# A fused attention, expert mixture and bilinear kernel on one Trainium2 core: the first expert in wider blocks, and a first list ordered against a clock

## The chip, the cores and the metric

One Trainium2 chip, one of its cores. The metric is the device time of one execution in microseconds; the kernel before was timed three times: 2153.72, 2157.41 and 2157.93, median 2157.41. Engines are called PE (TensorE, matmuls), DVE (VectorE), ACT (ScalarE), POOL (GpSimd) and SP (the queue that issues most DMAs).

## The reference

```python
def _attn_ref(q, k, v, f_logit):            # 4 batches, 8 heads, 768 steps, head size 48
    f = 1.0 / (1.0 + np.exp(-f_logit))
    for t in range(S):
        state = f[:, :, t, :, None] * state + np.einsum('bhd,bhe->bhde', k[:, :, t], v[:, :, t])
        y[:, :, t] = np.einsum('bhd,bhde->bhe', q[:, :, t], state)

def _moe_ref(x, w_gate, w1, w2):            # x: 3072 x 384, 8 experts, 1024 wide
    logits = x @ w_gate
    P = np.exp(logits - logits.max())
    for _ in range(8):
        P /= P.sum(1, keepdims=True) + 1e-09
        P /= P.sum(0, keepdims=True) + 1e-09
        P *= N / E
    for e in range(E):
        out += P[:, e:e + 1] * (np.maximum(x @ w1[e], 0.0) @ w2[e])

def _moe2_ref(x, w_a, w_b, w_out):          # 384 -> 1536 -> 384
    return (x @ w_a) * (x @ w_b) @ w_out
```

The three run one after the other: the attention's output, 3072 tokens of 384, is the mixture's x, and the mixture's output the bilinear layer's.

## The kernel before, in words

Everything is float32. A product is made of three matmuls: each operand is split in a part `hi` (a ScalarE copy into the type float32r) and what remains, `lo` (a subtraction on DVE or POOL), and the three are hi x hi, hi x lo, lo x hi. `gemm_f` (L508) is x times the first weights, `gemm_t` and `gemm_d` (L522, L533) are the second GEMM with the tokens or the model dimension on the output's partitions.

The program is two lists of operations. Each operation is put down by `Plan.add` (L106) with a priority, an engine, an estimated duration, the keys it reads and writes, and a function that issues its instructions; the list is then ordered by a planner that plays the engines through, and issued in that order. Each engine works off its own instructions strictly in that order.

The first list (`plan` of L596, ordered by `order`, L132, at L1150) holds 24 attention steps of 128 tokens (`attention`, L624), and as filler for PE the first expert without its last 128 hidden columns (`expert0`, L862): 7 hidden tiles, in blocks of 256 tokens (`EB`, L557). Block b can start when steps 2b and 2b+1 have left x as hi and lo (`b_x`, L575 to L580, two buffers). Per block the first GEMM is 7 x 9 matmuls of 256 columns; the second is 42 matmuls of 384 columns in blocks 0 to 3 and 63 of 256 columns in the others (`TURNED`). Each hidden tile leaves its PSUM bank by two ScalarE copies and one POOL subtraction (L875, L878, L880). `order` lets filler run on PE in a share of 0.6 to attention's matmuls. Until the first filler PE gets `spare` matmuls (L917) that compute nothing of use. Also in the first list: the splits of expert 0's weights (`add_piece`, L494: a DMA into one of two `raw` tiles, a ScalarE copy, a POOL subtraction), the gate's logits of one tile of 128 tokens (`logits`, L847: six matmuls with 16 or 8 columns), sums of x for the later stage (`x_make`, L1102), five x tiles (`x_take`, L1131), and the weights of the second list's jobs 0 and 1 (`w1_load`, `w1_split`, L1017 and L1047: raw blocks into `stage`, 13 sums, three splits into `w1t[0]` or `w1t[1]`).

The second list (`plan` of L1159, ordered by `timed`, L239) is the rest: the mixture's jobs and the bilinear layer's, 81 jobs of 45 matmuls of 512 columns in `front` (L1235), in 15 groups of three, and the second GEMMs in `back` and `back_turned`. `timed` plays its list through by `listed` (L270) with durations of its own, moves what held PE up to the front and keeps the best of 60 passes. At its start stand what the first list left of expert 0 (block 10's second GEMM and block 11), the last tile's logits, and the Sinkhorn rounds (`sinkhorn`, L929), eight times a matmul, a DVE column scaling (L960 to L962) and a row scaling. x tiles 9 to 14 and the hidden parts of later jobs share memory (`er`) with expert 0's tiles and wait for it by `guard`.

## Time and profile before

| | us |
|---|---|
| three timed runs | 2153.72, 2157.41, 2157.93 |
| profiled execution | 2153.39 |
| its span, first to last instruction | 2151.6 |
| PE busy | 2134.3 |
| DVE busy | 1720.0 |
| POOL busy | 1184.4 |
| ACT busy | 940.9 |

The profile is one execution of its own; its time stands beside its span, which leaves out what lies before the first and behind the last instruction. Busy times overlap. A matmul's own duration in a row is longer than what it costs, since matmuls run into each other: the distance from one row's start to the next is the cost.

### The profile page before, as it was taken

To read this page: it belongs to the slowest core of one execution; us is meant where nothing else is said; L and a number is where in the kernel's file an instruction comes from. 1 tells how busy PE (TensorE), PEld (TensorE's weight loads), DVE (VectorE), ACT (ScalarE), POOL (GpSimd) and SP (SyncE) were. 2 spreads that over 40 slices of the span, in tenths; PEclk is the share of its full clock that TensorE was granted. 3 is DMA by queue.
4 is the path that set the end of the run, shared out by engine and by line. 5 is a ranking of instruction groups with operands and counts; after the bars stand their busy time and mean duration, and the time that the engine had idled before them with its cause. 6 is when DMAs were issued, how large, how long until landed. Compare 5 with 4: busy or idle time off the path is not lost.

```text
span 2151.6 us, 41006 instructions
## 1 busy us (share of the span) xinstructions
PE 2134.3 (99%) x15371; PEld 1869.3 (87%) x15371; DVE 1720.0 (80%) x2882; ACT 940.9 (44%) x1761; POOL 1184.4 (55%) x1106
## 2 busy tenths in 40 slices
PE   8999999999999999999999999999999999999999
PEld 8999999989989999988888888888888888888888
DVE  7878888377878777698888986899998887866656
ACT  3544454454444445444444444444343445533331
POOL 2212121268877666477787767755545688535322
PEclk9999999999999999999999999999999999999999
DMA  6546644356675567865657678777665766878552
GB/s 133 116 106 165 166 112 98 109 203 241 235 254 196 185 223 267 279 227 194 219 179 232 198 273 279 243 255 247 226 199 174 239 218 228 302 232 283 172 173 74
DMA packets 340951, 438.66 MB, mean 204 GB/s; under 512 B 148024, under 2 KB 224656, under 8 KB 337296
## 3 DMA queue, kind: packets, MB, share of 16 engines
q1 hardware_dynamic: 326016, 422.40, 60.9%
q10 hardware_dynamic: 14736, 13.64, 1.9%
q8 instruction: 121, 1.98, 0.4%
q14 instruction: 78, 0.64, 0.1%
HBM read 295.58 MB, written 135.64 MB: 200 GB/s over the span
## 4 chain that ended last, share of the span: by engine, by line
PE 96%; DVE 3%; DMA 1%; issue 0%; ACT 0%; SPq 0%; DVEq 0%
PE pG L1258 28%; PE pR L539 21%; PE pR L528 18%; PE pF L1258 10%; PE pM L516 4%; PE pM L539 2%; PE pT L654 1%; PE pM L528 1%; PE pA L697 1%; PE pM L917 1%; PE pO L810 1%; PE pA L709 1%; PE pA L741 1%; PE pO L816 1%; PE pO L782 1%; DVE z L1539 1%
## 5 line engine op out<-in xcount | busy, mean ns | idle before, releaser
L539 PE MATMUL pR<-er 128*128 128x512 f32 (+1 forms) x2178 | 537.8, 383 | 0.0
L1258 PE MATMUL pG<-xs,w 128*128 128x512 f32 x1701 | 469.0, 392 | 3.6 <-DVE z L1539 3.0
L539 PEld LDWEIGHTS pR<-er 128*128 128x128 f32 x2178 | 401.1, 188 | 80.5
L528 PE MATMUL pR<-er 128*128 128x384 f32 x2232 | 433.8, 336 | 0.0
L1539 ACT ACTIVATE z<-pG 128x512 f32<-128x512 f32 x397 | 237.2, 598 | 437.5 <-PE pG L1258 370.5
L528 PEld LDWEIGHTS pR<-er 128*128 128x128 f32 x2232 | 397.6, 188 | 23.9
L1258 PEld LDWEIGHTS pG<-xs,w 128*128 128x128 f32 x1701 | 315.9, 188 | 64.3 <-DVE z L1539 3.2
L1539 POOL TENSOR_TENSOR er<-z,er 128x512 fp32r<-128x512 f32 x177 | 246.5, 1400 | 195.9 <-ACT er L1539 135.2
L1539 POOL TENSOR_TENSOR acc<-acc,tmp 128x512 f32<-128x512 f32 x168 | 232.4, 1390 | 173.3 <-DVE tmp L1539 172.3
L1539 ACT ACTIVATE er<-z 128x512 fp32r<-128x512 f32 x353 | 217.6, 628 | 212.4 <-PE pR L539 123.8
L1258 PE MATMUL pG<-er,w 128*128 128x512 f32 x972 | 276.5, 393 | 2.8 <-DVE z L1539 2.6
L1539 DVE TENSOR_TENSOR z<-pF,z 128x512 f32<-128x512 f32 x268 | 182.2, 684 | 64.4 <-PE pF L1258 42.8
L880 POOL TENSOR_TENSOR er<-l,er 128x256 fp32r<-128x256 f32 x84 | 74.6, 891 | 282.3 <-ACT l L878 234.5
L1258 PEld LDWEIGHTS pG<-er,w 128*128 128x128 f32 x972 | 180.9, 188 | 36.5 <-DVE z L1539 4.7
L1539 DVE TENSOR_TENSOR z<-z,pG 128x512 f32<-128x512 f32 x206 | 140.4, 682 | 63.5 <-PE pG L1258 61.9
L1539 POOL TENSOR_TENSOR stage<-stage 128x128 f32<-128x128 f32 x325 | 168.7, 551 | 19.8 <-DMA stage<-in_moe_w_dram 18.2
L1539 DVE SCALAR_TENSOR_TENSOR er<-z,er 128x512 fp32r<-128x512 f32 x150 | 146.6, 986 | 7.4 <-ACT er L1539 7.1
L1539 DVE SCALAR_TENSOR_TENSOR acc<-pR,prob,acc 128x384 f32<-128x384 f32 x168 | 100.5, 611 | 63.0 <-PE pR L528 60.6
L486 POOL TENSOR_TENSOR er<-raw,er 128x384 fp32r<-128x384 f32 (+1 forms) x82 | 94.4, 1159 | 101.8 <-ACT er L484 96.8
L1539 POOL TENSOR_TENSOR w<-stage,w 128x512 fp32r<-128x512 f32 (+2 forms) x75 | 125.0, 1677 | 38.4 <-ACT w L1539 33.5
L1258 PE MATMUL pF<-er,w 128*128 128x512 f32 x486 | 138.8, 394 | 0.0
L1258 PE MATMUL pF<-xs,w 128*128 128x512 f32 x486 | 136.8, 391 | 0.0
(283 smaller groups left out, 3227.0 us busy)
## 6 DMA issues: line engine op xcount, KB each, us to landing
er<-w2d SPq DMA_DIRECT2D x138, 384.0 KB, 4.4
wfmoe<-w SPq DMA_DIRECT2D x19, 1920.0 KB, 7.2
w<-wfmoe SPq DMA_DIRECT2D x38, 768.0 KB, 5.3
w2d<-er SPq DMA_DIRECT2D x69, 384.0 KB, 4.2
w<-wfmoe SPq DMA_DIRECT2D x38, 640.0 KB, 5.6
w<-wfmoe SPq DMA_DIRECT2D x38, 512.0 KB, 4.8
wfout<-w SPq DMA_DIRECT2D x8, 1920.0 KB, 7.7
raw<-in_moe_w_dram SPq DMA_DIRECT2D x64, 192.0 KB, 2.6
```

Of the source, the lines that this page charges most:

```text
L486: plan.add(prio + 1, "POOL", S_COST[0] + m * S_COST[1], [gk, key], [key], lambda: nc.gpsimd.tensor_tensor(out=lj, in0=got, in1=f32(hj), op ...
L516: nc.tensor.matmul(out=ps, lhsT=a[:, kk, fs], rhs=b[:, kk, :], start=(i == 0), stop=(i == 3 * KD - 1),)
L528: nc.tensor.matmul(out=ps, lhsT=a[:, off:off + 128], rhs=b, start=(start and i == 0), stop=(stop and i == n - 1))
L539: nc.tensor.matmul(out=ps, lhsT=a[:, d * 128:d * 128 + 128], rhs=b, start=(start and i == 0), stop=(stop and i == n - 1))
L654: nc.tensor.transpose(ps[0:R, p * 128:p * 128 + 128], src[:, p * 128:p * 128 + R], ident)
L697: nc.tensor.matmul(out=A0[o:o + 64, w, :], lhsT=pct(bk)[r, g, :], rhs=pct(bq)[r, g, :])
L709: nc.tensor.matmul(out=A1[o:o + 56, 0, w, :].rearrange("j (b e) -> j b e", e=8), lhsT=pct(k3)[r, g, 0:56], rhs=qv[r, g, :, 1, :])
L741: nc.tensor.matmul(out=A1[o:o + 48, 1, w, :].rearrange("j (b e) -> j b e", e=16), lhsT=pct(k3)[r, g, 0:48], rhs=qv[r, g, :, 1, :])
L782: nc.tensor.matmul(out=ps[64 * hd:64 * hd + m, p * D:(p + 1) * D], lhsT=kn[64 * c:64 * c + 64, p * R + 64 * hd:p * R + 64 * hd + m], rhs=b ...
L880: op(POOL, .76, [f"hh{ft}", kf], [f"hl{ft}"], lambda hh=hh, hl=hl, hf=hf: nc.gpsimd.tensor_tensor(out=hl, in0=hf, in1=f32(hh), op=ALU.subt ...
L1258: nc.tensor.matmul(out=ps, lhsT=a[:, slot], rhs=b, start=(new and i == 0), stop=(i == 2), skip_group_check=not new)
L1539: fn()
```

## The change

Expert 0's blocks are no longer all of 256 tokens: the first four are, then come four of 512 (`E0_BLOCKS`). x of a block lies in area p, q, p and q together, or r, which is the memory of x tiles 0 to 2 of the second list; the hidden tiles' lo part of a block of 512 lies in `w1t[1]`, the tile of job 1's weights. So job 1's weights move into the second list (on DVE), and x tiles 0 to 2 are taken when block 6 is through. Blocks 0 to 5 and block 6's first GEMM are in the first list, block 6's second GEMM and block 7 in the second. A block of 512 gives its first GEMM as operations of three matmuls, where an operation was nine.

The logits of blocks 0 to 6 are computed turned: the gate's 16 columns are the stationary operand, x the moving one (256 or 512 columns), six matmuls per block, then a ScalarE copy, one small transpose per tile and one reduction. Tiles 20 to 23 stay as they were.

Of expert 0's weights the second half of the first GEMM's is split after step 0 and the second GEMM's after step 1; their raw tiles are a ring of five (two `raw`, three parts of `stage`).

The first list's durations are new, and it is ordered by a function of its own, `first`, which plays it through with times per operation (`FIRST`), with POOL and some of DVE's operations as sharing a port, and places a spare matmul only where it fits before the next operation. The second list starts with each engine's lateness against PE at the first one's end (`late`).

```diff
+    def first(self, share, sooner):
...
+            if eng == "PE" and not ever:
+                while spares:
+                    cost = .215 if free[eng] < 8.0 else .12
+                    if free[eng] + cost > at + .05:
+                        break
...
+            turn = due >= 0.0
+            n = min((n for n in todo[eng] if ready[n] <= at + 1e-9), key=lambda n: (eng == "PE" and self.ops[n][6] != turn, prio[n]))
...
+            if n in self.shared and port - .03 > at:
+                at, other = port - .03, on_port
...
+    E0_BLOCKS = [(256, "p"), (256, "q"), (256, "p"), (256, "q"), (512, "r"), (512, "pq"), (512, "r"), (512, "pq")]
+    E0_LEFT = 1.5
+    LG_OLD = 7
+    W1_ON = "DVE"
+    W_AFTER = [], ["st0"], ["st1"]
...
+    ring_of = raw_of + stage_of
...
+    x_r = x_all[:, 0:3].rearrange("p a b -> p (a b)")
+    w_r = w1t[1].rearrange("p a b c -> p (a b c)")
...
+    areas = {"p": x_p, "q": x_q, "r": x_r, "h": h_p, "w": w_r}
+    owned = {"r": ["xs0", "xs1", "xs2"], "w": ["w110", "w111", "w112"]}
...
+    def h_of(b, ft):
+        n = e0_blocks[b][1]
+        lo = area("w", n * ft, n) if n == TB else area("h", n * (NF0 + ft), n)
+        return area("h", n * ft, n), lo
...
-    plan = Plan(same=.1, over=.07, ranked=True, early=2000, slack=.8)
+    plan = Plan(port=True)
...
+    def logits_turned(plan, b, prio, nm, bufs):
...
+        for i, (x, keys) in enumerate(((xH, kH), (xL, kL))):
+            def lg(i=i, x=x):
+                for kk in range(KD):
+                    nc.tensor.matmul(out=psl[0:2 * E, :n], lhsT=wgs[:, kk], rhs=x[:, kk], start=(i == kk == 0), stop=(i == 1 and kk == KD - 1))
+
+            plan.add(prio, PE, .681 if n == TB else .36, [*keys, *holds(b, True), "wgs"], [kl], lg)
...
+        def turn():
+            for j in range(m):
+                nc.tensor.transpose(psl[:, 2 * E * j:2 * E * (j + 1)], rt[0:2 * E, 128 * j:128 * j + 128], ident[0:2 * E, 0:2 * E])
...
-            op(PE, 1.08, xk + [f"e0i{ft // FT}{n}" for n in range(KD)], [km, "E0i"], lambda psm=psm, ft=ft: gemm_f(
-                psm[:, :EB], w_e0[ft // FT][0], ft % FT, b_x[b % 2]), 0.0, fill)
...
+            for kk in (range(KD) if n == TB else [None]):
+                op(PE, .681 if n == TB else 1.08, [*kH, *kL, *holds(b, True), *(wi if kk is None else wi[kk:kk + 1])], [km, "E0i"],
+                   partial(gemm_f, psm[:, :n], w_e0[ft // FT][0], ft % FT, (xH, xL), kk), 0.0, fill)
...
-        if i:
+        if i and block_of[i - 1] >= LG_OLD:
             logits(plan, i - 1, 1000 * i + 500, "O", p_O)
-        if i % 2 == 1 and i + 1 < NSTEP:
-            expert0(plan, i // 2, 1000 * (i + 1), "M", p_M, True, 0 if i + 3 > NSTEP - 1 else None)
+        b = block_of[i]
+        if b < LG_OLD and block_of[i + 1] != b:
+            logits_turned(plan, b, 1000 * (i + 1), "O", p_O)
+        if b < len(e0_blocks) - E0_LEFT and block_of[min(i + 1, NSTEP - 1)] != b:
+            expert0(plan, b, 1000 * (i + 1), "M", p_M, True, 0 if b + 1 > len(e0_blocks) - E0_LEFT else None)
...
-    for n in range(2):
+    for n in range(1 if e0_blocks[-1][1] == TB else 2):
         w1_load(plan, 1000 * (15 + 3 * n), n, [f"st{14 + 3 * n}"])
         w1_split(plan, 1000 * (15 + 3 * n) + 600, n, DVE)
     with tc.manual_schedule():
-        for fn in plan.order(SHARE):
+        plan.ranks()
+        for fn in plan.timed(partial(plan.first, SHARE), 1, 0):
             fn()
...
-    expert0(plan, NSTEP // 2 - 2, -8000, "R", p_R[:2], False, 1)
+    left = len(e0_blocks) - E0_LEFT
+    for x, b in enumerate(b for b in range(len(e0_blocks) - 1) if b + 1 > left):
+        expert0(plan, b, -8000 + 700 * x, "R", p_R[:2], False, 1 if b < left else None)
     logits(plan, NSTEP - 1, -4000, "R", p_R[:2])
-    expert0(plan, NSTEP // 2 - 1, E0_AT, "R", p_R[:2], False)
+    expert0(plan, len(e0_blocks) - 1, E0_AT, "R", p_R[:2], False)
     guard += ["E0i", "E0o", f"lg{NSTEP - 1}"]
+    if e0_blocks[-1][1] == TB:
+        w1_load(plan, -2000, 1)
+        w1_split(plan, -1000, 1, W1_ON)
```

The order that comes of it, at three places. First PE in the middle of the first list, around a tile's or a block's logits (pM are expert 0's PSUM banks, pO the logits', pA attention's; L516, now L602, is `gemm_f`; L854, now L973, the logits of a tile; L990 and L998 the turned ones and their transposes). Before:

```order
L516 MATMUL pM_167<-er 128x256 x9
L741 MATMUL pA_165<-q_136,k_138 48x32 x16
L516 MATMUL pM_166<-er 128x256 x9
L854 MATMUL pO_162<-wgs,er 128x16
L854 MATMUL pO_162<-wgs,er 128x8
L854 MATMUL pO_162<-wgs,er 128x16
L854 MATMUL pO_162<-wgs,er 128x8
L854 MATMUL pO_162<-wgs,er 128x16
L854 MATMUL pO_162<-wgs,er 128x8
L516 MATMUL pM_167<-er 128x256 x9
L752 MATMUL pA_165<-q_136,k_138 32x32 x16
```

Now:

```order
L602 MATMUL pM_162<-er 128x512 x3
L861 MATMUL pA_161<-q_132,k_134 48x32 x16
L990 MATMUL pO_158<-xs,wgs 16x512 x3
L602 MATMUL pM_162<-er 128x512 x3
L990 MATMUL pO_158<-xs,wgs 16x512 x3
L602 MATMUL pM_162<-er 128x512 x3
L872 MATMUL pA_161<-q_132,k_134 32x32 x16
L998 MATMUL pO_158<-ident,raw_78 128x16 x4
```

Nine matmuls of 256 columns between attention's became three of 512, and six matmuls and four transposes give the logits of four tiles.

Second, PE at the turn from the first list to the second (pR, pG and pF are the second list's banks; w_79 and w_80 are `w1t[0]` and `w1t[1]`, now w_75 and w_76; sk_m belongs to the Sinkhorn's start). Before:

```order
L516 MATMUL pM_166<-er 128x256 x9
L539 MATMUL pR_6603<-er 128x256 x21
L539 MATMUL pR_6604<-er 128x256 x21
L539 MATMUL pR_6603<-er 128x256 x21
L1258 MATMUL pG_6598<-xs_74,w_79 128x512 x3
L1258 MATMUL pG_6599<-xs_74,w_80 128x512 x3
L1258 MATMUL pF_6600<-xs_77,w_79 128x512 x3
L854 MATMUL pR_6604<-wgs,er 128x16
```

Now, from the last matmuls of expert 0's block 7:

```order
L624 MATMUL pR_5863<-w_76,er 128x512
L624 MATMUL pR_5863<-er 128x512
L1411 MATMUL pG_5857<-xs,w_75 128x512 x3
L1117 MATMUL pR_5864<-ident,prob 117x128
L1117 MATMUL pR_5864<-ident,prob 99x128
L1411 MATMUL pF_5861<-er,w_75 128x512 x3
L1411 MATMUL pG_5857<-xs,w_75 128x512 x3
L1411 MATMUL pG_5858<-xs,w_76 128x512 x3
```

Before, job 0 and job 1 alternate from the start, ahead of the last logits and the Sinkhorn; now expert 0's matmuls carry the Sinkhorn, whose last transpose (L1117) stands two groups ahead of job 1's first matmul.

Third, DVE at the splits of job 1's weights. Before they stand among attention's operations of the first list, now behind the Sinkhorn's last scaling (L1102). Before, then now:

```order
L677 TENSOR_TENSOR fi_129<-fi_129 112x128x2
L1152 TENSOR_TENSOR w_80<-stage,w_80 128x768
L677 TENSOR_TENSOR fi_129<-fi_129 112x128x2
L1152 TENSOR_TENSOR w_80<-stage,w_80 128x640
L720 TENSOR_TENSOR q_136<-q_136,g_151 112x16x16
```

```order
L1102 TENSOR_TENSOR prob<-prob,sk_c 128x24x8
L1697 TENSOR_TENSOR w_76<-stage,w_76 128x768
L1697 TENSOR_TENSOR z_5868<-pF_5859,z_5868 128x512
L1697 TENSOR_TENSOR w_76<-stage,w_76 128x512
L1697 TENSOR_TENSOR w_76<-stage,w_76 128x640
```

The three splits moved from attention's steps to the point where job 1's matmuls wait for them.

## Rows read from the trace of the kernel before

**Rows 1.** The page: busy time, share of the span and instructions of each engine.
```profile
PE 2134.3 (99%) x15371; PEld 1869.3 (87%) x15371; DVE 1720.0 (80%) x2882; ACT 940.9 (44%) x1761; POOL 1184.4 (55%) x1106
```

**Rows 2.** The page: the chain that ended last, share of the span by engine.
```profile
PE 96%; DVE 3%; DMA 1%; issue 0%; ACT 0%; SPq 0%; DVEq 0%
```

**Rows 3.** Busy time of each engine by stretch; columns in its first line.
```profile
core 0: us, PE busy (x) PEld busy (x) DVE busy (x) ACT busy (x) POOL busy (x), PEclk, DMA share, GB/s
0.00:55.17 55.17, 49.70 (x815) 46.89 (x816) 42.02 (x94) 19.62 (x39) 11.96 (x24) 1.00 0.63 134
55.17:409.20 354.03, 352.19 (x6344) 328.66 (x6342) 285.39 (x694) 169.75 (x417) 70.67 (x77) 1.00 0.51 120
409.20:471.00 61.80, 58.32 (x369) 52.03 (x364) 35.99 (x77) 33.80 (x73) 31.67 (x39) 0.97 0.50 172
```

**Rows 4.** PE's timeline, single rows: start us, us, engine line op out<-in xcount.
```profile
55.17 2.32 PE L516 MATMUL pM<-er 128*128 128x256 f32 x18
57.33 0.55 PE L763 MATMUL pO<-ident,k 112*128 112x112 f32 x4
57.66 1.33 PE L516 MATMUL pM<-er 128*128 128x256 f32 x9
58.88 0.65 PE L654 MATMUL pT<-ident,nat_q 128*112 128x128 f32 x4
...
405.39 0.83 PE L854 MATMUL pO<-wgs,er 128*128 128x16 f32 x6
406.08 1.31 PE L516 MATMUL pM<-er 128*128 128x256 f32 x9
...
409.27 5.65 PE L516 MATMUL pM<-er 128*128 128x256 f32 x45
414.76 7.89 PE L539 MATMUL pR<-er 128*128 128x256 f32 x63
422.49 1.55 PE L1258 MATMUL pG<-xs,w 128*128 128x512 f32 x6
423.88 0.84 PE L1258 MATMUL pF<-xs,w 128*128 128x512 f32 x3
...
1008.93 0.84 PE L1258 MATMUL pF<-er,w 128*128 128x512 f32 x3
1009.61 0.84 PE L539 MATMUL pR<-er 128*128 128x512 f32 x3
```

**Rows 5.** PE by line, 55.17 to 409.2: expert 0's groups.
```profile
L516 PE MATMUL pM<-er 128*128 128x256 f32 x648 | 93.5, 291 | 0.0
L539 PE MATMUL pM<-er 128*128 128x256 f32 x378 | 56.7, 293 | 0.0
...
L528 PE MATMUL pM<-er 128*128 128x384 f32 x168 | 35.6, 350 | 0.0
```

**Rows 6.** The start: spare matmuls by line, DVE's timeline, its group by line.
```profile
L917 PE MATMUL pM<-er 128*128 128x256 f32 x193 | 28.5, 304 | 3.1 <-DVE er L916 3.1
...
20.10 1.75 DVE L701 TENSOR_TENSOR q<-bq,fi 112x512 f32<-112x512 f32 x1
...
L701 DVE TENSOR_TENSOR q<-bq,fi 112x512 f32<-112x512 f32 x21 | 14.8, 706 | 5.2 <-DMA xf<-q 5.0 <-issue 0.2
```

**Rows 7.** DVE's groups and longest wait in the middle, then POOL's sums (page).
```profile
L1152 DVE TENSOR_TENSOR stage<-stage 128x128 f32<-128x128 f32 x26 | 6.2, 284 | 2.5 <-DMA stage<-in_moe_w_dram 2.5
L1152 DVE TENSOR_TENSOR w<-stage,w 128x768 fp32r<-128x768 f32 (+2 forms) x6 | 5.0, 826 | 0.0
L859 DVE TENSOR_REDUCE logit<-pO 128x8 f32<-128x16 f32 x22 | 3.6, 166 | 0.5 <-PE pO L854 0.5
...
DVE S L801 <- PE pO L782: 9.6, 11, 2.5
...
L1539 POOL TENSOR_TENSOR stage<-stage 128x128 f32<-128x128 f32 x325 | 168.7, 551 | 19.8 <-DMA stage<-in_moe_w_dram 18.2
```

**Rows 8.** The turn: PE's and DVE's timelines, and engines by stretch.
```profile
458.86 1.65 PE L1258 MATMUL pG<-er,w 128*128 128x512 f32 x3 [2.61 <-DVE z L1539]
463.98 0.93 PE L1258 MATMUL pG<-xs,w 128*128 128x512 f32 x3 [0.87 <-DVE z L1539]
468.83 0.38 PE L977 MATMUL pR<-ident,prob 128*117 128x128 f32 x2
...
456.23 1.98 DVE L962 TENSOR_TENSOR prob<-prob,sk_c 128x192 f32<-128x192 f32 x1
...
459.00:460.00 1.00, 1.00 (x3) 0.81 (x4) 0.93 (x4) 0.00 (x0) 0.34 (x1) 0.50 0.98 417
460.00:462.00 2.00, 2.00 (x7) 1.71 (x6) 1.81 (x5) 1.35 (x3) 0.00 (x0) 0.50 1.05 436
```

More of the change, by code (lines that the diff above doesn't have):

```diff
@@ L987 @@
     for i in range(NSTEP):
+        if i == 0 and not W_AFTER[0]:
+            e0_weights(0, False, [])
         attention(i)
+        if i == 0 and W_AFTER[0]:
+            e0_weights(0, False, W_AFTER[0])
+        if i == 1:
+            for u, outs, after in ((1, False, W_AFTER[1]), (0, True, W_AFTER[2]), (1, True, W_AFTER[2])):
+                e0_weights(u, outs, after)
         if i == 0:
```

373 lines of the change are left out of this document (231 added, 142 removed).

## The prediction

> **What bounds the kernel now.** I read the page's busy line first: TensorE (PE) is busy for 2134.3 of 2151.6 us [rows 1], so whatever shortens the kernel must take work or idle time from PE. Then the chain that ended last: 96% of it is PE, 3% VectorE (DVE) [rows 2]. Then the same numbers by stretch, cut where the program changes [rows 3]: up to 55.17 us the pipeline fills (PE's 193 spare matmuls hide how long it really waits), from 55.17 to 409.20 attention and expert 0 share PE, which is idle for only 1.8 us of 354.0, from 409.20 to 471.00 the first list ends and the second starts, with 3.5 us idle. So in the first 471 us PE's own work sets the time, and the change is to be costed by the PE time of what it issues. DVE is the next engine: 285.4 of the 354.0 us, that is, 68.6 us idle.
>
> The profiled execution took 2153.4 us; the median of the three timed runs is 2157.4, 4.0 above it. I work out differences from the profile and add them to the median.
>
> **Prices.** A row of the timeline followed by the next row's start gives what PE really spends. 45 matmuls of 256 columns in one go: 409.27 to 414.76, 122 ns each; 63: 414.76 to 422.49, 122.7 ns [rows 4]. Nine of them between attention's matmuls: 57.66 to 58.88, 1.22 us, 135 ns each; so a change between attention and expert 0 costs 1.22 - 9 x 0.122 = 0.12 us. Of 512 columns: six in 1.39 us (422.49 to 423.88) and, later, three in 0.68 us (1008.93 to 1009.61): 227 to 232 ns, I take 229 [rows 4]. Two of 256 cost 245 ns where one of 512 costs 229: the same columns are 16 ns cheaper.
>
> **Expert 0 in the first list.** Before: 693 matmuls of the first GEMM (11 blocks) and 378 of the turned second GEMM, all of 256 columns [rows 5], the last 45 of the 693 in one go behind 409.2 [rows 4]: 648 x 0.135 + 45 x 0.122 + 378 x 0.135 = 144.0 us. The 168 of 384 columns are the same before and after. The new order keeps 252 of 256 columns (34.0 us) and has 315 of 512, in 82 pieces: 315 x 0.229 + 82 x 0.12 = 82.0 us. Together 116.0: **-28.0 us**. The matmuls of 512 columns among attention's are not in the trace. Lower bound: no cost of a change, 72.1 us for them (gain 38); upper: each piece of three at 0.69 + 0.12 us, 270 ns, 85 us (gain 25). I take 82, since the change was measured on the same attention matmuls. About 21 us of the 28 are moved work, 7 are columns that got cheaper.
>
> **Logits.** A tile's six small matmuls take 0.69 us (405.39 to 406.08 [rows 4]); 23 tiles stand in the first list: 15.9 us. Now a block of 256 costs six matmuls of 256 in two pieces (0.73 + 0.12) and two transposes (four like them take 0.33 us, 57.33 to 57.66 [rows 4]; 0.17 and a change, 0.12): 1.14 us, four of them 4.6; a block of 512 six matmuls (1.37 + 0.24) and four transposes (0.33 + 0.12): 2.06, three of them 6.2; three tiles remain the old way, 2.1. Sum 12.9: **-3.0 us**. The seven added ScalarE copies and the reductions lie beside PE; ScalarE is busy for 170 of 354 us [rows 3].
>
> **Start.** The first matmul of expert 0 stands at 55.17 us [rows 4], behind 193 spare matmuls, 28.5 us in all [rows 6]; the new order has 157 ahead of its first. 36 x 0.148 = 5.3 us, if the chain through DVE is really that much shorter; nothing, if the same waits come back as idle time. DVE's order there is nearly the same, but ten of the thirteen splits of expert 0's weights on GpSimd (POOL) now wait for step 0 or 1, and beside such splits DVE's own instructions were long (1.75 us where the same instruction's mean is 0.71 [rows 6]). **-2.5 us**, between 0 and -5.3.
>
> **Second list.** Before: 63 + 126 matmuls of 256 columns, 189 x 0.1225 = 23.1 us. After: 189 of 512, 43.3 us. All of it is on the path, since PE is the bound there: **+20.2 us**.
>
> **DVE.** Its work in the middle stretch falls by job 1's share of the weights (half of 6.2 + 5.0 us) and some of the logits' reductions (3.6 us for 22) [rows 7], about 7.6 us, while PE's falls by 31: DVE would be busy for 278 of some 323 us, 86% instead of 81%. Its waits for PE (9.6 us for the state update alone [rows 7]) shrink if PE comes sooner; some will turn up as PE waiting for DVE. **+2 us**, from 0 to +25 (all the squeezed idle time returns).
>
> **The turn between the lists.** Job 1's six loads, 13 sums and six splits (three on ScalarE, three on DVE) move behind the second list's start, past the Sinkhorn rounds. The split into its tile must wait for expert 0's last matmul, and PE's first matmul of job 1 stands three matmul groups (3 x 0.69) and two transposes (0.4) behind that: about 2.4 us, against one ScalarE copy and one DVE split (mean 0.83 us [rows 7]). Behind them job 2's loads wait for the staging tile: 13 sums on POOL at 0.55 us and the splits make some 15 us from expert 0's end [rows 7], and PE has 21 groups of 0.69 and four of 0.5 us before it needs them, 17. Now PE loses 2.61 + 0.87 us in waits for DVE there, and the granted clock is 0.50 for the 3 us behind the longer wait, so that three matmuls take 1.65 us instead of 0.86 [rows 8]: another 1.7 us. The wait began while DVE's column scaling took 1.98 us beside POOL, and stood between the Sinkhorn rounds [rows 8]; in the new order the rounds lie under expert 0's 43 us and the fronts behind them, with DVE full. I take **0**, between -5.2 and +5.
>
> Sum: -28.0 - 3.0 - 2.5 + 20.2 + 2 + 0 = -11.3 us. 2157.4 - 11.3 = **2146 us**.
>
> **A rule against it.** The rows make 504 matmuls of 512 columns (315 + 189) cheaper by 504 x 0.016 = 8.1 us than the same columns in 1008 of 256. By the Trainium skill, page "TensorE: Matmul & The Clock Gate", section "Back-to-back issue gap", a warm matmul costs its columns plus some six cycles: 262 cycles for 256 columns, 518 for 512. By that rule joining two saves 2.6 ns, an estimate of 1.3 us for the 504, and the sum would be about -4.5 us. The trace has 122.5 ns for 256 columns, more than that page's 109, so I go by the rows.
>
> **Rivals.**
> 1. *Joining saves nothing among attention.* If a matmul of 512 columns costs two of 256 in these streams, 8.1 us are lost: 2154 us. Against it: both kinds were timed in rows of the same GEMMs [rows 4]. Chance 0.05. By the rule of the Trainium skill told above (page "TensorE: Matmul & The Clock Gate", section "Back-to-back issue gap") it would nearly be so.
> 2. *DVE paces part of the first list.* If a third of the 25 us by which DVE's idle time must shrink comes back as PE's waits, +8: 2154 us. For it: 86% busy, in order, and with sums and x tiles in the last steps. Chance 0.14.
> 3. *DVE keeps all its waits (slower).* The middle stretch is then 278 + 68.6 = 346 us, shorter by 7.6 us alone, while the second list pays 20.2: -7.6 - 2.5 + 20.2 = +10, 2167 us. It decides once PE's idle time in the middle grows by over 13 us. Against it: DVE's longest waits now are for PE [rows 7], and those end sooner. Chance 0.06.
> 4. *The turn closes too.* No wait of over 1 us and no half clock at the turn, and the start gains its full 5.3: -5.2 - 2.8: 2138 us. Chance 0.12.
>
> **How the numbers follow.** My forecast has 0.63, with its own range 2140 to 2152 (the bounds of the fill, -10 and +3, seldom met in full; the start, +-2.7; the turn, +-5, not all at once). 80% reaches from 2135 (rival 4 and a little) to 2157 (rivals 1 and 2), and leaves out rival 3. A measurement tells 0.2%, 4.3 us, from no change. Faster by more: the forecast, rival 4, and under half of rivals 1 and 2, which lie at the edge: 0.63 + 0.12 + 0.06 = 0.81; within 0.2%: 0.12; slower: rival 3 and mishaps, 0.07.
>
> **What would show it.** Right: the last attention step's output matmuls end near 371 us instead of 409 (expert 0 has 51 of its matmuls behind them then, 11.7 us, where 45 of 256 were 5.5); expert 0's first matmul between 50 and 55; matmuls of 512 columns in the first list at 229 ns in a row, about 0.8 us per piece of three; DVE at 85 to 88% between, PE still above 98%; some 64 us from there to the Sinkhorn's last transpose, where 409.27 to 468.83 are 59.6 now [rows 4, 8], and job 0's and 1's front matmuls mostly behind it. Wrong: PE idle by over 5 us in the middle with DVE named as releaser (rivals 2, 3), 245 ns a matmul of 512 (rival 1), or waits for the weights of job 1 or 2 at the turn with the granted clock at 0.50 behind them.

## The result, and the profile after

| | before | changed |
|---|---|---|
| timed runs, median us | 2157.56 (2153.72 to 2157.93, 4 runs) | 2171.45 (2170.38 to 2172.79, 4 runs) |
| ratio, 95% interval | | 1.0069 (1.0051 to 1.0086) |
| profiled execution's span | 2151.6 | 2170.3 |

The change makes the kernel slower by some 14 us, where I had forecast 11 us less. The two profiled executions are further apart, 18.8 us (2172.21 - 2153.39), because the profile of before is of one of its quicker executions. The page of the changed kernel, its busy line and the chain that ended last (before: [rows 1, 2]):

```profile
PE 2139.8 (99%) x14773; PEld 1835.9 (85%) x14773; DVE 1728.2 (80%) x2869; ACT 937.6 (43%) x1700; POOL 1175.5 (54%) x1078
...
PE 91%; DVE 5%; DMA 2%; issue 1%; ACT 1%; SPq 0%; POOL 0%; DVEq 0%; ACTq 0%; POOLq 0%
```

598 matmuls fewer, and PE is busy for longer all the same; its share of the chain falls from 96 to 91%, and those of DVE, DMA, ScalarE and issue rise. The stretches, cut at expert 0's first matmul and attention's last output matmul, as in [rows 3], and at the second list's first matmul:

```profile
core 0: us, PE busy (x) PEld busy (x) DVE busy (x) ACT busy (x) POOL busy (x), PEclk, DMA share, GB/s
0.00:58.15 58.15, 49.58 (x774) 46.31 (x774) 40.85 (x92) 18.84 (x38) 10.34 (x22) 0.88 0.63 135
58.15:402.44 344.29, 330.98 (x5775) 279.89 (x5775) 271.95 (x660) 153.71 (x348) 53.53 (x50) 0.97 0.50 116
402.44:414.75 12.31, 12.31 (x58) 10.28 (x59) 1.71 (x3) 7.56 (x14) 5.85 (x5) 1.00 0.13 33
```

Two things are new. PE is idle for 13.3 of the 344.3 us (344.29 - 330.98), where it was 1.8 of 354. And PEclk stands at 0.97 there and 0.88 before, where both were 1.00. What a matmul at half clock loses I count as PE's busy time times (1 - PEclk), taken from a table by slices of 1 us: 10.1 us in the middle, 6.4 us ahead of it. So the span's 18.7 us come out as

| | before | changed | difference | forecast |
|---|---|---|---|---|
| up to expert 0's first matmul | 55.2 | 58.2 | +3.0 | -2.5 |
| from there to the second list: PE's work at full clock | 357.7 | 333.1 | -24.6 | -31.0 |
| PE idle there | 1.8 | 13.3 | +11.5 | +2 |
| lost at half clock there | 0.0 | 10.1 | +10.1 | no term |
| second list | 1736.8 | 1755.5 | +18.7 | +20.2 |
| sum | 2151.6 | 2170.3 | +18.7 | -11.3 |

Where the idle time comes from is read in three views. PE's longest waits of the first 600 us (us in all, times, longest) and DVE's between 58 and 376 us:

```profile
PE pA L861 <- DVE k L842: 7.7, 3, 3.9
PE pT L774 <- DMA nat_f<-in_f_logit_dram: 7.3, 2, 4.5
...
DVE xr L1303 <- DMA xr<-x1d: 11.1, 5, 3.7
DVE q L821 <- DMA xf<-q: 8.3, 5, 2.8
```

The timelines of DVE and of PE around the first of these waits, and one row of each around another:

```profile
178.83 0.63 DVE L797 TENSOR_TENSOR fi<-fi 112x256 f32<-112x256 f32 x1
181.72 1.19 DVE L1303 TENSOR_TENSOR xr<-xr,xr 128x512 f32<-128x512 f32 x1 [2.26 <-DMA xr<-x1d]
182.84 0.59 DVE L797 TENSOR_TENSOR fi<-fi 112x256 f32<-112x256 f32 x1
183.35 0.68 DVE L1303 TENSOR_TENSOR xr<-xr,xr 128x512 f32<-128x512 f32 x1
183.96 0.41 DVE L840 TENSOR_TENSOR q<-q,g 112x256 f32<-112x256 f32 x1
184.29 0.41 DVE L842 TENSOR_TENSOR k<-k,g 112x256 f32<-112x256 f32 x1
...
323.06 0.69 DVE L1303 TENSOR_TENSOR xr<-xr,xr 128x512 f32<-128x512 f32 x1 [3.75 <-DMA xr<-x1d]
...
179.56 1.31 PE L602 MATMUL pM<-er 128*128 128x256 f32 x9
184.75 1.17 PE L861 MATMUL pA<-q,k 48*48 48x32 f32 x32 [3.89 <-DVE k L842]
185.86 1.10 PE L774 MATMUL pT<-ident,nat_k 128*112 128x128 f32 x4
...
324.48 0.77 PE L861 MATMUL pA<-q,k 48*48 48x32 f32 x26 [3.43 <-DVE k L842]
```

DVE stands 2.26 us before a sum of x for the second list, which nobody needs yet, because its x has not landed. Behind it in DVE's order stand the scaling of attention's q and k (L840, L842), and PE, whose next instruction needs them, waits 3.89 us. At 323 us the same comes again, 3.75 us of DVE and 3.43 us of PE. Then the clock falls, and stays at half (1.2 GHz) for 6 us after this wait, and behind three others likewise:

```profile
29.00:41.00 12.00, 11.94 (x167) 11.04 (x169) 5.79 (x16) 2.92 (x6) 0.00 (x0) 0.50 0.76 156
186.00:192.00 6.00, 6.00 (x63) 5.05 (x64) 3.72 (x13) 2.31 (x7) 0.00 (x0) 0.50 0.48 105
288.00:294.00 6.00, 6.00 (x78) 4.75 (x77) 4.57 (x15) 2.38 (x4) 0.00 (x0) 0.50 0.69 184
326.00:331.00 5.00, 5.00 (x56) 3.94 (x54) 1.24 (x4) 1.59 (x3) 1.26 (x1) 0.50 0.65 184
```

The DMA issues between 150 and 330 us (issues, KB each, median us from issue to landing):

```profile
xr<-x1d SPq DMA_DIRECT2D x13, 256.0 KB, 4.1
```

The changed planner takes 0.4 us for the issue and 2.5 us (`LATE`) for the way of this load, 2.9 us in all; it takes 4.1. Before, the planner had 0.4 + 4.0 and 0.8 us that `order` adds, 5.2, and DVE waited for these loads for 2.1 us in all. By the Trainium skill, page "DMA: Bandwidth & Descriptors", section "Anatomy of one DMA — SWDGE (gpsimd) path", a DMA issued on that path costs some 2.0 us and its bytes by 436 GB/s, an estimate of 2.6 us for 256 KB. SP issued the loads here, so no run shows what that fit is worth on its own path.

The start has one such wait too, for step 2's f (SP's timeline, then PE's):

```profile
15.49 4.44 SPq L590 DMA_DIRECT2D stage<-in_moe_w_dram  x6
19.98 3.78 SPq L721 DMA_DIRECT2D wg<-in_moe_w_gate_dram  x6
23.88 0.51 SPq L590 DMA_DIRECT2D raw<-in_moe_w_dram  x1
24.48 0.38 SPq L590 DMA_DIRECT2D stage<-in_moe_w_dram  x1
24.96 1.77 SPq L757 DMA_DIRECT2D nat_f<-in_f_logit_dram  x1
...
29.06 1.10 PE L774 MATMUL pT<-ident,nat_f 128*112 128x128 f32 x4 [2.77 <-DMA nat_f<-in_f_logit_dram]
```

With five raw tiles nothing holds the weight loads back, and they stand on SP ahead of a load that PE needs.

### The profile page after: what moved, and what is told of

Same layout as the page of the kernel before. It is cut to its first block, busy times and chain, and to the rows that moved or that the text cites. A ratio compares the mean times of both kernels' runs of the same rounds, so it can differ in the third digit from the quotient of the medians.

```text
span 2170.3 us, 39625 instructions
## 1 busy us (share of the span) xinstructions
PE 2139.8 (99%) x14773; PEld 1835.9 (85%) x14773; DVE 1728.2 (80%) x2869; ACT 937.6 (43%) x1700; POOL 1175.5 (54%) x1078
## 4 chain that ended last, share of the span: by engine, by line
PE 91%; DVE 5%; DMA 2%; issue 1%; ACT 1%; SPq 0%; POOL 0%; DVEq 0%; ACTq 0%; POOLq 0%
PE pG L1411 27%; PE pR L624 21%; PE pR L613 18%; PE pF L1411 10%; PE pM L602 3%; PE pM L624 2%; PE pT L774 2%; PE pM L613 1%; PE pO L930 1%; PE pO L902 1%; PE pA L861 1%; PE pA L817 1%; DVE z L1697 1%; PE pO L936 1%; PE pA L829 1%
## 5 line engine op out<-in xcount | busy, mean ns | idle before, releaser
L624 PE MATMUL pR<-er 128*128 128x512 f32 x2136 | 550.3, 390 | 0.0
L1697 DVE SCALAR_TENSOR_TENSOR er<-z,er 128x512 fp32r<-128x512 f32 x150 | 157.8, 1058 | 15.0 <-ACT er L1697 13.3
L1697 DVE TENSOR_TENSOR z<-pG,z 128x512 f32<-128x512 f32 x145 | 99.5, 686 | 37.7 <-PE pG L1411 35.6
L1303 POOL TENSOR_TENSOR w<-l,er 128x512 fp32r<-128x512 f32 x21 | 29.4, 1398 | 179.4 <-ACT l L1303 179.4
```

The costliest lines, as they stand in the source:

```text
L624: nc.tensor.matmul(out=ps, lhsT=a[:, d * 128:d * 128 + 128], rhs=b, start=(start and i == 0), stop=(stop and i == n - 1))
L1303: fn()
L1697: fn()
```

## The experiments

The cause was sought between two theories. Theory A: loads are planned shorter than they are, DVE stands in order behind them, PE waits, and the clock behind each wait doubles the price. Theory B: DVE, in order and at 86% by the forecast (79% in the changed kernel's middle stretch, 272.0 of 344.3 us), has too little slack for blocks that give PE less to do. In each kernel's spans the work of PE between expert 0's first matmul and the second list, its idle time and what half clock takes are counted as above; lines of a kernel with added lines lie one or more further on.

| kernel | us | ratio to before, 95% | PE work | idle | half clock |
|---|---|---|---|---|---|
| x_late | 2155.91 | 0.9993 (0.9980 to 1.0005) | 334.3 | 8.7 | 0.0 |
| all_late | 2158.97 | 1.0006 (0.9996 to 1.0015) | 333.5 | 8.5 | 8.4 |
| w_early | 2170.95 | 1.0063 (1.0046 to 1.0080) | 335.2 | 14.2 | 12.1 |
| blocks256 | 2199.13 | 1.0189 (1.0165 to 1.0213) | 362.7 | 21.7 | 15.9 |
| before_short | 2166.80 | 1.0040 (1.0027 to 1.0053) | 358.8 | 6.0 | 3.0 |
| blocks256_x | 2172.91 | 1.0072 (1.0058 to 1.0085) | 365.4 | 9.0 | 1.7 |
| x_late_nat2 | 2152.62 | 0.9989 (0.9974 to 1.0004) | 334.0 | 9.6 | 11.9 |
| old_order | 2194.86 | 1.0172 (1.0159 to 1.0185) | 330.1 | 24.0 | 26.4 |
| slack | 2169.94 | 1.0064 (1.0047 to 1.0081) | 331.7 | 14.1 | 9.7 |
| slack_dve | 2156.68 | 1.0005 (0.9994 to 1.0015) | 332.6 | 8.4 | 9.9 |
| job0_pool | 2151.65 | 0.9984 (0.9971 to 0.9997) | 336.5 | 6.5 | 0.0 |
| lg_old | 2176.24 | 1.0093 (1.0078 to 1.0108) | 341.8 | 13.6 | 13.5 |
| noshift | 2171.09 | 1.0068 (1.0050 to 1.0085) | 333.7 | 14.0 | 8.3 |
| x_shift | 2166.15 | 1.0043 (1.0025 to 1.0060) | 334.7 | 14.0 | 11.9 |
| n_shift | 2169.56 | 1.0060 (1.0046 to 1.0074) | 332.5 | 10.1 | 13.5 |
| xn_shift | 2168.18 | 1.0052 (1.0034 to 1.0071) | 335.2 | 12.3 | 1.7 |
| x_replan | 2161.78 | 1.0022 (1.0011 to 1.0032) | 335.6 | 10.0 | 1.7 |
| xn_replan | 2161.32 | 1.0021 (1.0010 to 1.0031) | 335.2 | 11.6 | 0.0 |

The us are medians of 4 to 12 executions, the last three columns belong to the profiled one alone, which need not be a typical one (x_late_nat2: 2162.73 beside a median of 2152.62; x_shift: 2175.62 beside 2166.15). Three chips were used, each kernel beside the kernel before (medians of 2154.9 to 2157.4), so the ratio is the fairer column to compare by. The column of PE's work is steady, 330 to 337 us for all kernels with the new blocks and turned logits, 358 to 365 with blocks of 256, before's included. What moves the time is mostly in the two columns behind it. The second list, which the table leaves out, moves it as well: with the new blocks it took 1751.1 to 1757.8 us (1755.5 in the changed kernel).

### x's loads taken for longer

```diff
     LATE = 2.5
+    X_LATE = 6.0
...
-                plan.add(prio, SP, .4, [kx], [key], partial(nc.sync.dma_start, out=t, in_=src), LATE)
+                plan.add(prio, SP, .4, [kx], [key], partial(nc.sync.dma_start, out=t, in_=src), X_LATE)
...
```

and the same for the loads of `x_take`.

> Edit: in the changed kernel, the planner takes 6.0 us instead of 2.5 us for the first list's loads of x for the sums (x_make, x_take); nothing else. Theory A (loads planned too short: DVE stands in order behind a sum whose x has not landed, attention's scaling stands behind it, PE waits 3.4 to 3.9 us and then runs at half clock for 6 to 7 us): DVE's 11.1 us of waits for xr fall below 3 us, none of PE's waits between 58 and 402 us is over 1.5 us, the granted clock is 1.00 there, and the time is 2171 - (8 of waits + 9 of half clock) = 2154, within 2150 to 2161. Theory B (DVE has too little slack at 86% whatever it waits for: the same idle time comes back under another name): DVE waits elsewhere, PE still idle for over 9 us in the middle, 2166 to 2173.

2155.91, within A's range and 15.5 us below the changed kernel. DVE's waits for these loads, and the middle:

```profile
DVE xr L1304 <- DMA xr<-x1d: 0.7, 1, 0.7
...
55.44:382.69 327.25, 318.59 (x5760) 269.59 (x5760) 273.38 (x660) 152.84 (x345) 53.43 (x49) 1.00 0.53 122
```

11.1 us of waits became 0.7, and the clock is 1.00 throughout. One wait of PE of 2.8 us is left, for ScalarE, where theory A allowed none over 1.5. Of the 19.4 us between the two profiled executions the stretch from expert 0's first matmul to the second list gives 13.7 (10.1 of half clock and 4.7 of idle time, less 1.1 of PE's work), the start 2.7 and the second list 3.0. But this number reorders the whole first list, so that more than these waits may have changed.

### Attention's loads too

```diff
-                out=b_nat[nm][z][:, :, 0:D], in_=src[b, :, t0:t0 + 128, :].rearrange("h t d -> t h d")), 2.7)
+                out=b_nat[nm][z][:, :, 0:D], in_=src[b, :, t0:t0 + 128, :].rearrange("h t d -> t h d")), 5.0)
```

and 3.0 to 5.0 for v, 1.8 to 4.0 for Y, on top of x_late.

> Edit: as x_late, and the planner takes 5.0, 5.0 and 4.0 us for attention's loads of f, q, k, of v and of Y (2.7, 3.0 and 1.8 in the changed kernel). Theory A: besides what x_late gains, the 2.8 us wait for nat_f at 29 us and the 13 us of half clock behind it go, worth some 9 us: 2145, within 2140 to 2152. Theory B: 2163 to 2173. A third way: loads that are taken to be longer raise their rank alone, SP's order hardly moves at the start, and the wait at 29 us stays: then as x_late.

2158.97: a miss of all three. The wait for step 2's f goes, one of 3.0 us for ScalarE at 20 us takes its place, expert 0 begins at 55.1, and the middle has waits of 1.5 to 2.3 us for DVE and ScalarE with half clock behind. Longer loads everywhere are not better.

### The weights as they came before

```diff
-    W_AFTER = [], ["st0"], ["st1"]
+    W_AFTER = [], [], []
...
-    ring_of = raw_of + stage_of
+    ring_of = raw_of
```

> Edit: in the changed kernel, expert 0's weights again go through two raw tiles in place of five and are split as they come (no waiting for step 0 or 1). Theory A (start: SP issues weight loads into the five raw tiles and the gate's six ahead of step 1's f, so PE waits 2.8 us at 26 us and runs at half clock for 13 us): SP issues f of step 1 before 20 us again, no half clock before 58 us, expert 0's first matmul at 52 to 56 us instead of 58, the time 2171 - 3 to 7 = 2164 to 2168, if the middle's waits stay as they are. Rival: the start is bound by DVE, which the splits on POOL make slower; then the first matmul stays at 57 to 59 us and the time within 2168 to 2175.

The start did what theory A says: first matmul at 55.15, no half clock up to it. The time did not: 2170.95, the rival's, since the middle has 14.2 us idle and 12.1 lost at half clock. The start's 3 us were not where the 14 us are.

### The new order with the old blocks, and the old order with the new ones

```diff
-    E0_BLOCKS = [(256, "p"), (256, "q"), (256, "p"), (256, "q"), (512, "r"), (512, "pq"), (512, "r"), (512, "pq")]
+    E0_BLOCKS = [(256, "p"), (256, "q")] * 6
...
-    LG_OLD = 7
+    LG_OLD = 0
```

and the two edits of w_early.

> Edit: the changed kernel's list with the blocks of before (twelve of 256 tokens, logits of one tile at a time, job 1's weights in the first list, two raw tiles, weights split as they come). So what is left of the change is the first list's order and its durations. Theory A (the new order plans loads too short): the order alone loses time, DVE waits over 6 us for xr, PE has waits of over 2 us with half clock behind, time 2163 to 2175, over before by 5 us or more. Theory B (the blocks take the work away under which DVE's waits lay): PE is idle by under 4 us in the first 400 us, no half clock, 2153 to 2160.

2199.13, far beyond what I expected of either theory: 21.7 us idle, seven places of half clock. DVE waited 12.7 us for xr. In this kernel expert 0's hidden copies have one buffer where before had two halves, and PE waits for those as well (1.8, 1.4 and twice 0.7 us), so it is not the kernel before with another order alone. With x's loads at 6.0 us, as in x_late:

> blocks256 with x's loads planned at 6.0 us as in x_late. If the planned load time is all that is wrong with the new order, this falls by over 25 us, to 2155 to 2172; if the new order loses time with blocks of 256 for another reason (in blocks256 PE waits for expert 0's hidden copies and for DVE elsewhere too), it falls by some 10 us only: 2183 to 2195.

2172.91, 26 us less from the one number, the largest effect of it, though just outside the range; 16 us above before remain, and PE is still idle for 9.0 us. The mirror, in the kernel before, with its own order and blocks:

```diff
     LATE = 4.0
+    X_LATE = 1.7
...
```

> The mirror of x_late: the kernel before, with the planner's time for the first list's loads of x (x_make, x_take) cut from 4.0 to 1.7 us, which with the 0.8 us that its order adds is the 2.5 us of the changed kernel. Theory A (a planned time below what the load takes sets DVE's order wrong, whatever the blocks): DVE waits over 6 us in all for xr (2.1 now), PE has one to three waits of over 1.5 us in the middle with half clock behind, 5 to 15 us slower: 2162 to 2172. Rival (before has enough filler and slack to swallow it): DVE's waits for xr grow, PE's do not, 2155 to 2160.

2166.80, 10 us slower, as theory A has it. DVE waits longer for x (2.1 us before, [rows 7] show its other waits), and PE's middle stretch takes 361.75 us where it took 354.03 [rows 3]:

```profile
DVE xr L1153 <- DMA xr<-x1d: 13.6, 6, 4.6
...
60.60:422.35 361.75, 355.78 (x6339) 330.96 (x6337) 283.38 (x693) 169.35 (x417) 72.11 (x77) 0.99 0.50 117
```

The profiled execution also lost 5.4 us ahead of expert 0, where its instructions are those of before in the same order: PE waited 2.6 us for a split on POOL at 19 us, and the clock stood at half for some 14 us behind it, which took 6.8 us. So of the 13.9 us between the two profiled executions the edit accounts for the middle's 7.7. Last, the changed kernel's blocks, ordered by the function of before, with x's loads at 4.0 us (`X_LATE`); the operations' durations are the changed kernel's, and before's `over=.07`, which takes 0.07 us off each operation of DVE and ScalarE, is left out:

```diff
-    plan = Plan(port=True)
+    plan = Plan(same=.1, ranked=True, early=2000, slack=.8, port=True)
...
-        plan.ranks()
-        for fn in plan.timed(partial(plan.first, SHARE), 1, 0):
+        by_order = plan.order(SHARE)
+        plan.timed(partial(plan.first, SHARE), 1, 0)
+        for fn in by_order:
             fn()
```

> The changed kernel's blocks, logits and weights, its first list ordered by the function of before (with 0.8 us added to every load and wait between engines) and x's loads at 4.0 us as before. If the loss lies in what the new function takes loads for, and not in it playing the list against a clock, this is about as x_late: 2150 to 2162. If the blocks starve the order of filler and DVE of slack whichever function orders it: 2162 to 2175. If the timed order has a worth of its own: x_late stays 5 us or more ahead.

2194.86: 24.0 us idle, 26.4 lost at half clock. With these blocks the old order is worse by 39 us than the timed one with x's loads mended, so the loss is not the timed order as such. I read it as the blocks leaving filler up to attention's end only if it is dealt out evenly (here it ends 1.2 us behind attention, in x_late 15.7); that was not tested, nor the old order with the durations of before.

### Step 2's loads first, more slack, less for DVE, the logits

These five kernels stand on x_late; x_late_nat2 has one more line, which the other four keep:

```diff
-        self.ops = [(o[0] if o[0] == 10 ** 9 else -r - 10 ** 4 * (o[0] < 2000), *o[1:]) for o, r in zip(self.ops, rank)]
+        self.ops = [(o[0] if o[0] == 10 ** 9 else -r - 10 ** 4 * (o[0] < 2009), *o[1:]) for o, r in zip(self.ops, rank)]
```

> x_late, and step 2's loads join the first class of ranks (priorities below 2009 instead of 2000), so that SP issues step 2's f behind the first weight load instead of behind nine weight loads and the gate's six. If these weight loads are what PE's 4.05 us wait at 26 us comes from: that wait and the 4 us of half clock behind it go, expert 0's first matmul comes at 50 to 53 us instead of 55.4, and the time is 2156 - 3 to 6 = 2150 to 2153. Rival: DVE's chain of steps 0 and 1 is as late anyway, the wait becomes one for DVE or ScalarE, and the time stays within 2153 to 2160.

2152.62, within the range; x_late's interval (0.9980 to 1.0005) and this one's (0.9974 to 1.0004) overlap, so the gain over x_late is not clear. Its twelve executions tell more than their median: five had a mean granted clock of 1.000 over the whole span and took 2148.1 to 2152.0, three had 0.993 to 0.996 and took 2161.3 to 2163.9. The same program, some 13 us apart, by how often half clock came.

```diff
-                way = late if late else 0.0 if eng == to == "SP" else self.AGAIN[eng] if eng == to and eng != "PE" else 0.0 if eng == to else self.WAY.get(eng, 0.0) + .05
+                way = late if late else 0.0 if eng == to == "SP" else self.AGAIN[eng] if eng == to and eng != "PE" else 0.0 if eng == to else self.WAY.get(eng, 0.0) + .3
```

> x_late_nat2, and the first list's function takes 0.3 us instead of 0.05 us on top of the way from one engine to another. Theory A2 (what is left, some 8 us of PE waits of 0.3 to 2.8 us for DVE and ScalarE in x_late, is the plan being exact to a tenth of a microsecond while the chip is not, so that filler stands a little too early or too late): PE's waits between 55 us and attention's end fall below 5 us in all and the time to 2143 to 2150. Rival (DVE's own work sets it, at 86% and in order; a looser plan only moves the waits): waits stay at 7 to 12 us, 2150 to 2158.

```diff
+            if eng == "DVE":
+                cost += .05
```

> x_late_nat2, and the first list's function takes every DVE operation to be 0.05 us longer. By theory A2 PE is given more filler between attention's steps and waits less: 2144 to 2151. Rival: the plan then believes DVE to be the bound, attention stretches and filler runs out before attention ends: 2153 to 2165.

2169.94 and 2156.68, the second within the rival's range: planning looser does not help. With 0.3 us on every way between engines attention ends at 413.0, 1.2 us before the second list; there is no filler left and DVE waits 22.7 us for attention's own DMA (xf) instead. Theory A2 falls, in these two forms.

```diff
-        w1_split(plan, 1000 * (15 + 3 * n) + 600, n, DVE)
+        w1_split(plan, 1000 * (15 + 3 * n) + 600, n, POOL)
```

> x_late_nat2 with the 13 sums and three splits of job 0's weights in the first list on POOL instead of DVE (13 x 0.28 + 2.5 = 6 us less for DVE). If DVE's load is what is left of the loss: PE's waits in the middle fall by 3 us or more, 2146 to 2150. If it is where single waits happen to stand: no change beyond 2 us, 2150 to 2155; and if POOL beside DVE slows DVE's own instructions, 2155 to 2160.

2151.65, the only kernel here whose interval lies below before's time, and barely (0.9984, 0.9971 to 0.9997); 1 us beside x_late_nat2 is what I had called no change. Its profiled execution took 2148.55 and never saw half clock; its middle:

```profile
52.59:384.37 331.78, 325.37 (x5783) 273.14 (x5781) 268.40 (x643) 155.50 (x347) 67.17 (x67) 1.00 0.52 121
```

6.4 us idle are left there, against 9.6 in x_late_nat2's (whose profiled execution took 2162.73) and 8.7 in x_late's. So the mark of 3 us less in waits is met by the one and not by the other, and whether DVE's load is what is left stays open.

```diff
-    LG_OLD = 7
+    LG_OLD = 0
```

> x_late_nat2 with the logits of one tile at a time as before (this part of the change undone alone). My term for turning them is 3.0 us of PE time: the time rises to about 2155.6, 2153 to 2159, and PE's busy time for logits up to attention's end from some 12.9 to 15.9 us. Rival (turning them costs PE as much in waits for x's split and the copy as it saves; x_late_nat2 waits 2.5 us in all for L991's and L999's operands): 2150 to 2153.

2176.24, where I had 2155.6. PE's work is 7.8 us more than in x_late_nat2, not 3.0, and the profiled executions differ by 4.0 us of idle time and 1.6 of half clock as well. Either the turned logits are worth several times their matmuls, since each tile's six matmuls are one more thing for PE, pO's banks and DVE to agree on, or this is a list that falls badly. One run does not tell.

### Single moves in the changed kernel's own order

Since a number in the planner moves everything, these kernels take the changed kernel's order and move single instructions by a sort that keeps all the others (PE's order is the same to the instruction in all of them).

```diff
+        by = {n: plan.when[n][0] + moved(n) for n in sorted(plan.made)}
...
+            if eng == "DVE" and key[:2] == "xr":
+                return 4.0
+            if eng == "SP" and key == "natf0" and turn == 2:
+                return -8.0
```

> The changed kernel again, every engine's instructions in the same order, beside the three below on the same chip: 2170 to 2173. Its profile is a second execution of the same program: by theory A DVE's waits for xr and PE's waits of 3 to 4 us behind them come at the same places; how long the clock stays at half behind each may differ.

2171.09: the changed kernel again. In its second profile the waits stand at the same places (3.38, 1.27 and 3.16 us at 181, 286 and 323 us), but expert 0 begins at 55.37, not 58.15, since half clock behind the start's 2.8 us wait lasted 3.4 us, not 13.6. So only about 0.2 of the start's 3.0 us belong to the program.

> The changed kernel's own order with one thing moved: DVE's 14 sums of x in the first list (L1303, into xr) stand where the plan has them 4 us later, and what depends on them follows. PE's order is the same to the instruction; no other DVE instruction changes its place against another. Theory A: DVE's 11.1 us for xr fall below 4 us, PE's waits at 181, 287 and 321 us shrink below 1 us or go, with the half clock behind them: 8 of waits + 9 of half clock, so 2154 to 2160. Theory C (x_late gained by the whole list falling otherwise, the sums were incidental): 2166 to 2173.

> The changed kernel's own order with one DMA moved: step 2's load of f stands on SP ahead of four weight loads into stage, the gate's six and two more weight loads; nothing else changes on any engine. If those loads are what PE's 2.8 us wait at 26 us comes from, it goes, with the 13 us of half clock behind it (or as much of it as comes of that wait), and expert 0's first matmul stands at 51 to 55 us instead of 58: 2163 to 2168. Rival: ScalarE or DVE is next in the chain and as late: less than 2 us, 2169 to 2172.

> Both moves, x_shift and n_shift. If the two losses are separate, the gains add: 2148 to 2155, and less than 8 us of half clock in the first 400 us. What then is left against my forecast of 2146 is PE's short waits for DVE and ScalarE.

2166.15, 2169.56 and 2168.18: theory A in this form falls, and the two gains do not add. In x_shift and xn_shift the waits named are gone (DVE waits for xr no more), and others took their place; n_shift, which moved f alone, keeps 10.2 us of DVE's waits for xr. SP, ScalarE and PE in xn_shift:

```profile
324.02 4.64 SPq L952 DMA_DIRECT2D xf<-q  x6
...
330.55 0.52 ACT L964 ACTIVATE xs<-xf 128x384 fp32r<-128x384 f32 x1 [7.24 <-DMA xf<-q]
...
332.68 0.59 ACT L1327 ACTIVATE l<-pM 128x512 f32<-128x512 f32 x1
...
333.33 1.09 PE L604 MATMUL pM<-er 128*128 128x512 f32 x3 [3.95 <-DMA x1d<-xf]
```

SP issues in order as well. Behind the stores of the later sums stood attention's own DMA (xf); it was issued late, ScalarE stood 7.24 us in front of its copy of xf, expert 0's hidden copy out of PSUM (into l) came behind that, and PE waited 3.95 us. The profile names a DMA as what ended PE's wait; I read it as the bank, since the copy ends at 333.27 us and the matmul starts at 333.33. At the start PE waited 2.1 us (n_shift) and 2.4 us (xn_shift) for q where it had waited for f. A wait handed from one queue in order to the next is no wait removed. So the whole chain of x was moved, on all its engines:

```diff
...
+            if key[:2] == "xr" or key[:3] == "xf0" or (key[:2] == "xs" and any(plan.key.get(d, "")[:2] == "xr" for d in deps)):
+                by[n] = max([by[n]] + [ends[d] + .2 for d in deps if d in ends])
+                ends[n] = by[n] + takes + (3.5 if eng == "SP" and key[:2] == "xr" else 3.0 if eng == "SP" else 0.0) + (2.5 if eng == "SP" and key[:2] == "xr" else 0.0)
...
```

> x_shift mended: in x_shift SP stood in order behind the stores and loads that wait for the later sums, so attention's own loads (xf) came late and PE waited 2.8 to 4.0 us for ScalarE at 333 to 344 us instead. Here the whole chain of x (loads, sums, stores, takes) is put at the times that follow if a load takes 6 us to land; every other instruction of the changed kernel keeps its place, PE's order is the same to the instruction. Theory A (the few misplanned waits are the loss): no wait of PE over 1.5 us between 58 us and attention's end, 2154 to 2161. Theory C (the waits only change their place while PE's order stays: with so little slack on DVE, ScalarE and SP the whole list has to be planned with them): 2163 to 2170, with other waits of 1 to 3 us and half clock behind them.

> x_replan, and step 2's loads of f, q and k stand on SP ahead of the gate's six and three weight loads (n_shift moved f alone, and PE then waited 2.1 us for q). Theory A: the wait at 26 to 29 us goes too, 3 to 5 us on top of x_replan: 2150 to 2157. Theory C: 2160 to 2168.

2161.78 and 2161.32. The middle of x_replan, to be held against the changed kernel's:

```profile
55.59:390.61 335.02, 325.07 (x5775) 274.08 (x5775) 272.27 (x660) 153.53 (x348) 55.80 (x50) 0.99 0.52 120
```

The same 5775 matmuls in the same order take 335.0 instead of 344.3 us, and the medians differ by 9.3 us too (2171.09 to 2161.78). That lies between what the theories gave, and one wait of 1.7 us (for ScalarE, at 330 us) is over theory A's 1.5. Against noshift, PE's idle time falls from 14.0 to 10.0 us and half clock's share from 8.3 to 1.7. So x's chain, planned too early, is shown to cost two thirds of the 14 us by which the change is slower; the last third is not explained by it. Step 2's loads, put right on top, gained 0.5 us: another wait (3.09 us for DVE at 44.8 us) took their place.

## Why the prediction was wrong

**Expert 0's work, -28.0: right in kind, short in size.** 45 + 378 + 648 matmuls of 256 came to 144.1 us by starts in the trace of before, where I had 144.0. Of the new ones 48 of 512 in a row take 11.0 us, 229 ns each:

```profile
402.37 0.96 PE L602 MATMUL pM<-xs,er 128*128 128x512 f32 x3
403.17 0.72 PE L973 MATMUL pO<-wgs,er 128*128 128x16 f32 x6
403.75 11.15 PE L602 MATMUL pM<-xs,er 128*128 128x512 f32 x48
414.75 0.39 PE L624 MATMUL pR<-er 128*128 128x512 f32 x1
```

and a piece of three among attention's 0.80 (402.37 to 403.17), as forecast. Two of 256 cost 245, so rival 1 is out. The rule that I weighed gives 216 ns, by the Trainium skill, page "TensorE: Matmul & The Clock Gate", section "Back-to-back issue gap" (518 cycles at 2.4 GHz), which gives it for an isolated matmul, where I took it for matmuls in a row; in a row the trace does not agree, with 229. In x_late, whose clock is full in the middle, the rows from start to start give 83.9 us for the 315 (forecast 82.0), 34.2 for those of 256 (34.0), and 1.2 us more for the 168 of 384. What I had left out: attention's own matmuls get dearer, those of the state (L782, L903 in x_late) from 17.9 to 20.8 us; they stand in 56 runs where they stood in 43, which is the cause as I read it and was not tested. Together PE's work fell by 23.4 us in x_late, 24.6 in the changed kernel, not by 31.0.

The split of the 28 us that I gave, 21 of moved work and 7 of cheaper columns, does not follow from my own price: 315 x 0.016 is 5.0. The sum does not hang on it.

**Logits, -3.0**: -3.2 in x_late by the same rows. Undone alone (lg_old) this part costs 24 us, and why is open.

**Start, -2.5**: +3.0 in the one execution, +0.2 in the other. In the first of them PE had 6.5 us less of work there, and 3.1 us of idle time and 6.4 us lost at half clock took it back, most of it in and behind the wait for step 2's f. I had looked at DVE's order there and not at SP's.

**Second list, +20.2**: +18.7, which hides two misses of opposite sign. PE's work there grew by 21.7 us, and 3.1 us of idle time and half clock went. The turn closed, as in the first half of rival 4: no wait of over 1 us and a clock of 1.00 there, where before lost 3.5 us idle [rows 3] and 1.7 at half clock [rows 8]; 1.7 us of short waits are left up to 480 us. Attention's end to the Sinkhorn's last transpose is 64.5 us (402.44 to 466.98), where I had 64.

**DVE's waits, +2: this step failed.** I argued that DVE's waits for PE shrink when PE comes sooner, and that its slack, 68.6 us, is squeezed by 25 (by my own figures 31 - 7.6, 23.4). DVE's busy time came near what I said (272 us, forecast 278). But a mean share of 79 to 86% says nothing of an engine that works in order: five sums waiting for x for 11.1 us stood in front of what PE needed next, and 7.3 of PE's 13.3 idle us are the two waits shown above for the scaling behind them. PE's idle time rose by 11.5 us, inside my bounds of 0 to 25, though I took 2, and the sign that I had named came: PE idle by over 5 us with DVE as releaser. The mechanism is that of rival 3: DVE was idle for 72.3 us in the middle (344.3 - 272.0), no less than the 68.6 before. Its price was 2167 for waits that all come back; I gave it 0.06, because I read DVE's longest waits of before, which are for PE [rows 7], and not what the change does to the waits for loads. That could be read before: the diff has `LATE = 4.0` become 2.5, and in the trace of before the 13 loads of xr landed 3.7 us after their issue (median; the longest of the eight whose landing the trace has, 4.9).

**Half clock, no term.** I had seen 1.7 us of it at the turn [rows 8] and gave it no price where new waits come. It took 10.1 us, nearly as much as the waits themselves (8.3 us in the second execution).

Either of the last two alone carries the time above 2157, the end of my range: 2171.5 less the 10.1 us of half clock is 2161, with the waits at +2 and half clock as it was 2162, and only without both 2152. Attention's last output matmul shows the same: at 402.4 us, where I had 371, some 31 us late, of which the start has 5.5, PE's work 6.4, the waits 9.5 and half clock 10.1.

**Open.** With x's loads mended the forecast still does not come: x_late's profiled execution is 10.6 us above before's less 11.3, 7.5 of it by PE's work, 4.8 by waits and 2.8 by the start, less 4.5 in the second list. x_late is 6 us ahead of x_replan, which has the changed kernel's order of PE. Of the 9.8 us between their profiled executions 5.3 stand in the second list (1752.5 and 1757.8 us), 4.4 in the middle; what in the two orders makes either was not separated. Even the best kernels keep 6 to 10 us of short waits in the middle, for DVE and ScalarE alike: what theory B may have right, and about what my rival 2 had as 8 us. And why half clock follows one wait and not another: in x_late a wait of 2.8 us at 215 us has none behind it, in the changed kernel one of 1.0 us at 287 us has 6 us.

## What to carry to other kernels

When a change takes filler from the engine that sets the time, the question is not whether the others' busy share still fits, but what stands at the head of each queue in order: list what each can wait for there, loads above all, and compare the planned time of each with its landing time in the trace. A wait is priced with the half clock that may follow it, here about as much again. And a single misplaced operation is mended on all the queues that it passes through, SP's among them; moved on one engine alone, the wait comes out at the next.
